# Mixture-of-experts kernel on one core: first layers of experts 1, 2 and 4 by seven products, and the weights' sums on GpSimd

## The chip, the cores and the metric

The kernel runs on one core of a Trainium2 chip. A core has five engines, each with an instruction queue of its own that it works through strictly in order: TensorE (PE in the profile, its weight loads PEld), VectorE (DVE), ScalarE (ACT), GpSimd (POOL) and SyncE (SP, which here only issues DMAs). The metric is the device time of one execution in microseconds. The result must equal the reference in float32.

## The reference, cut to what matters

```python
# attention block: r, k, v of shape (4, 8, 768, 48), w and u of shape (8, 48)
for t in range(S):
    cur = einsum('bhd,bhe->bhde', u[None] * kt, vt)
    y[:, :, t] = einsum('bhd,bhde->bhe', rt, state + cur)
    state = w[None, :, :, None] * state + einsum('bhd,bhe->bhde', kt, vt)
x = y.transpose(0, 2, 1, 3).reshape(3072, 384)          # 3072 tokens, D = 384

# experts: w_gate (384, 8), w1 (8, 384, 1024), w2 (8, 1024, 384)
for idx in argsort(-(x @ w_gate).flatten()):            # greedy, best score first
    tok, e = idx // 8, idx % 8
    if assigned[tok] < 0 and counts[e] < 384:           # each expert takes exactly 384 tokens
        assigned[tok] = e; counts[e] += 1
for e in range(8):
    h = maximum(x[assigned == e] @ w1[e], 0)            # first layer: 384 x 384 @ 384 x 1024
    out[assigned == e] = h @ w2[e]                      # second layer: 384 x 1024 @ 1024 x 384
```

## The kernel before, in words

The attention part runs first, to about 140 us, on all engines. The rest is the experts' part, and the change lies there. Every matmul is float32, and the trace shows a float32 matmul as two MATMUL records with a weight load each.

**Order of the experts.** Experts are numbered in the order in which the greedy assignment fills them up. A part of expert 0's tokens is worked on early, beside the end of the attention part; then the method `run` takes experts 1 to 7, one after the other, and the remaining tokens of expert 0 last. For each expert `run` holds `ahead`: its number, its gathered tokens, its token list, `w1` and `w2`.

**The search for the next expert.** `later()` is a generator that finds which expert is filled next and with which tokens. It is pulled in pieces by `progress`, at fixed fractions of the current expert's work (`due`), so its instructions are written in among the expert's own. It does three rounds of `count`: VectorE builds an indicator `ind` from the scores (L936), TensorE counts with it in three matmuls into `counts` (L948), VectorE reduces them to `own`, `cnt` and `wide`, one more matmul (L959) spreads the count over all partitions, and VectorE takes `most`, `full`, `dg`, `cand` and `low` from it. After the third round come the marks `acc`, their sums on TensorE (`st_ps`, L1079 and L1080), then the token lists (`some_ps`, L1412, and `list_ps`, L1430). `load_weights` has SP issue the loads of `w2` and `w1` as soon as the expert is known, and `gather` (L1518) has GpSimd issue three indirect DMAs for its tokens. `turn` (L1533) transposes the gathered tokens to `xT` on TensorE.

**First layer.** `hidden` is the plain one: 8 blocks of 128 hidden units by 3 chunks of D, 24 matmuls of 384 columns (48 in the trace), each block then passed through ScalarE's ReLU into `hid`. `hidden_by_seven` (matmuls at L1601) uses seven products instead of eight for a 2 by 2 blocking (Strassen's scheme in Winograd's form) of the first two chunks of D. For it `weight_sums` forms four sums of `w1`, `first_T1` to `first_T4` of 128 x 512 (L1548), and `row_sums` five sums of `xT`, `first_S1` to `first_S5` of 128 x 192 (L1559), all on VectorE. Inside it ScalarE copies three kinds of products out of PSUM (`keep`) and VectorE adds six pairs (`added`, each with one operand in PSUM). `FIRST_BY_SEVEN = 3, 6, 7` names the experts that use it. For such an expert the sums of `w1` are written when the expert before it stands at `t > 1.1`, that is in its second layer, and the sums of `xT` right behind the transposes.

**Second layer.** Experts 1 to 5 use `seven` (matmuls at L1698), with `seven_w2` for four sums of `w2`, `T1` to `T4` of 128 x 768 on VectorE (through `sums_of`, L1673), and `S1` to `S4` of `hid`, also through `sums_of` and of 768 elements. Experts 6 and 7 (`many`) use fifteen products, with `fifteen_w2` through `sums_of`. A third block of rows is done plainly in `result` (L1756), and `scatter` (L1750) has GpSimd write rows out by indirect DMA.

**What sets the order.** The instructions of the experts' part are put in order by a scheduler from the order in which the code is written, from what they depend on and from modelled durations; the order of each engine is then fixed. `late` is true for the first expert of `run` only: there `seven_w2` is held behind the first half's sum `S3` by `tc.issue_after`. It also goes to `hidden` as `lead`, where the first two blocks then go token block by token block.

Of the kernel before, what the change touches and what calls it, by code (L numbers as in the profile page):

```python
# [1452 lines left out]
def rwkv5_eagle_then_base_layer_balanced(  # L1453
# [12 lines left out]
    nc = tc.nc  # L1466
    N, DX = out.shape
    E, _, F = moe_w1.shape
    NT = N // 128
    CAP = N // E  # L1470
    NC = CAP // 128
# [14 lines left out]
    ADD, SUB = ALU.add, ALU.subtract  # L1486

    class Experts:
# [49 lines left out]
            *_, xT = self.turned(ahead, lambda c: self.ps_t.tile([128, KD, 128], F32, name="xT_ps"))  # L1538
            return xT

        def weight_sums(self, w1):
            H = F // 2
            at = {f"b{2 * k + f}": w1[:, k, ts(f, H)] for k in range(2) for f in range(2)}
            at.update({f"c{f}": w1[:, 2, ts(f, H)] for f in range(2)})
            for name, a, op, b in (("T1", "b1", SUB, "b0"), ("T2", "b3", SUB, "T1"), ("T3", "b3", SUB, "b1"),
                                   ("T4", "b2", SUB, "T2")):
                t = self.first.tile([128, H], F32, name=f"first_{name}")
                nc.vector.tensor_tensor(out=t, in0=at[a], in1=at[b], op=op)  # L1548
                at[name] = t
            return at  # L1550

# [110 lines left out]
        def seven_w2(self, w2):  # L1662
            H, D = KF // 2, DX // 2
            at = {f"w{2 * j + k}": w2[:, ts(j, H), ts(k, D)] for j in range(2) for k in range(2)}
            self.sums_of(at, (("T3", "w3", SUB, "w1"), ("T1", "w1", SUB, "w0"), ("T2", "w3", SUB, "T1"),
                              ("T4", "w2", SUB, "T2")), D)
            return at

        def sums_of(self, at, which, n=128):
            for name, a, op, b in which:  # L1670
                kind = f"sum_{name[0] in 'TW'}_{sum(k[0] in 'TWSH' for k in at)}"
                t = self.sums.tile([128, KF // 2, n], F32, name=name, tag=kind)
                last = nc.vector.tensor_tensor(out=t, in0=at[a], in1=at[b], op=op)  # L1673
                at[name] = t
            return last

# [85 lines left out]
            nc.scalar.copy(o_sb, o_ps)  # L1762
            self.scatter(o_sb, tok[:, c:c + 1], to)

        FIRST_BY_SEVEN = 3, 6, 7

        def run(self, ahead, later, rows, pulls={}, xT=None):
            xT, lead = xT or self.turn(ahead), True
            row_sums = weight_sums = None
            while ahead:  # L1770
                n, _, tok, w1, w2 = ahead
                nb = tok.shape[1]
                whole = nb == NC
                many = whole and n in (E - 2, E - 1)
                sums = dict(row_sums or {}, **weight_sums) if weight_sums else None
                row_sums = weight_sums = None
                ahead = next((a for a in later if a), None)
                after = ahead and ahead[0] in self.FIRST_BY_SEVEN and ahead[2].shape[1] == NC
                late, lead = lead and not many, False
                right = (self.fifteen_w2 if many else self.seven_w2)(w2) if whole and not late else None  # L1780
                left = {}
                some = pulls.get(n, 2)
                due = [1.55, 1.75] if some == 2 else [0.75 + 1.15 * i / (some - 1) for i in range(some)]

                def half(hid):
                    nonlocal right
                    for name, (i, j) in self.BLOCKS.items():
                        left[name] = hid[:, ts(j, KF // 2), ts(i, 128)]
                    if many:
                        return  # L1790
                    last = self.sums_of(left, self.SEVEN_EARLY)
                    if late:
                        with tc.issue_after(last.ins):
                            right = self.seven_w2(w2)

                def turn():
                    nonlocal xT, row_sums
                    if ahead:
                        xT = self.turn(ahead)
                        if after:  # L1800
                            row_sums = self.row_sums(xT)

                def progress(t):
                    nonlocal weight_sums
                    if after and t > 1.1 and not weight_sums:
                        weight_sums = self.weight_sums(ahead[3])
                    while due and t > due[0]:
                        due.pop(0)
                        next(later, None)
                        if many and not due:  # L1810
                            turn()

                def at_product(part):
                    progress(1 + part)

                if sums:
                    hid = self.hidden_by_seven(sums, sums, progress)
                    half(hid)
                else:
                    hid = self.hidden(w1, xT, nb * 128, half if whole else lambda hid: None, progress, late)  # L1820
                if many:
                    self.sums_of(left, self.HID_SUMS)
                    self.fifteen(left, right, tok, rows, at_product)
                    continue
                if whole:
                    self.sums_of(left, self.SEVEN_LATE)
                    self.seven(left, right, tok, rows, at_product, turn)
                for c in range(NC - 1 if whole else 0, nb):
                    if c == nb - 1 and not whole:
                        turn()  # L1830
                    self.result(c, hid, w2, tok, next(rows))
# [34 lines left out]
    with ExitStack() as whole:  # L1866
# [6 lines left out]
        with ExitStack() as part:  # L1873
# [20 lines left out]
            with tc.manual_schedule():  # L1894
                one, last = mild.run(step)
# [26 lines left out]
                ahead = 1, xg, to, *have["v"]  # L1922
# [6 lines left out]
                for m in (0, 1, 99):  # L1929
                    go(m)  # L1930
                    xT = next(turned)
# [87 lines left out]
```

## Time and profile before

| what | value |
|---|---|
| median of 3 runs | 394.73 us (394.64 to 395.28) |
| profiled execution | 393.36 us, of it 391.6 from the first to the last instruction |
| granted TensorE clock | 0.995 |
| TensorE, VectorE, ScalarE, GpSimd busy | 96%, 72%, 43%, 36% of the span |
| 0 to 140 us: the same four | 134.1, 99.1, 104.9, 90.0 us |
| 152.4 us to the end (239.2 us): the same four | 231.1, 171.8, 62.5, 47.3 us |
| first layer of experts 1 to 7 starts at | 152.4, 185.9, 218.6, 250.1, 283.2, 315.3, 344.9 us |
| rest of expert 0 starts at | 374.1 us |

The two rows by time show the two halves of the kernel: the attention part, where all engines are busy, and the experts' part, where TensorE is busy for nearly all of the time. Starts are those of the first matmul of the stage on TensorE. The profiled execution is one run of the program; the median is over other runs.

A row of the timeline reads: start, duration in us, engine, line, operation, output <- inputs, partitions x elements of one row; in brackets the idle time ahead of it and what ended that. A row of the groups or of one line's instructions has the count, shortest, median and longest duration in ns, and the first and the last start. In the waits, "VectorE own <- PE counts: 5.3, 7, 2.8" is 5.3 us in all, 7 times, 2.8 at most. In the windows each engine has its busy us and its count of instructions; behind them stand the granted clock, the share of DMA and the GB/s.

### The profile page before, as it was taken

Reading aid. Unit: us, or ns where it says so; the run is one execution under the profiler, and the core shown is the slowest. Engines: PE = TensorE matmul, PEld = TensorE weight load, DVE = VectorE, ACT = ScalarE, POOL = GpSimd, SP = SyncE. Lnnn points to the kernel's source line nnn. Section 1 sums busy time; section 2 is a strip of 40 time slices with the busy share of each in tenths; the row PEclk is TensorE's granted clock in tenths of the full one; section 3 lists DMA queues with packets and bytes.
Section 4 is the critical chain, followed back from the end, with each engine's and each line's share of the span. In section 5 each row is a group of like instructions: output and inputs, shape, how many; then the busy total and the mean of one; then the engine's idle time right before and its main releaser. Section 6 shows DMA issues by size and latency. Waiting matters only on the chain. (4 is left out here: it accounts for less than half of the span.)

```text
span 391.6 us, 9858 instructions
## 1 busy us (share of the span) xinstructions
PE 377.2 (96%) x3777; PEld 306.2 (78%) x3777; DVE 281.4 (72%) x959; ACT 169.3 (43%) x452; POOL 141.2 (36%) x173
## 2 busy tenths in 40 slices
PE   8899999999999999999999999999999999999992
PEld 7677888888877866687578899558657889989991
DVE  6755777586885788985949949888378976994530
ACT  4997989888883311312222242121222234234220
POOL 7878887767732022032122021203203212070020
PEclk9999999999999999999999999999999999999997
DMA  9999999988692164651560560109209264280010
GB/s 121 160 180 174 210 189 201 174 171 157 129 338 82 43 241 181 195 190 42 164 238 28 168 251 20 41 5 345 77 20 338 85 231 173 52 329 24 2 62 27
DMA packets 95335, 57.35 MB, mean 146 GB/s; under 512 B 77232, under 2 KB 89520, under 8 KB 95280
## 3 DMA queue, kind: packets, MB, share of 16 engines
q1 hardware_dynamic: 91936, 47.21, 48.0%
q0 software_dynamic: 3104, 9.44, 7.0%
q8 instruction: 31, 0.51, 0.6%
q14 instruction: 24, 0.20, 0.2%
q10 hardware_dynamic: 240, 0.00, 0.0%
HBM read 47.20 MB, written 9.44 MB: 145 GB/s over the span
## 5 line engine op out<-in xcount | busy, mean ns | idle before, releaser
L1624 PE MATMUL h_ps<-xT,w 128*128 128x384 f32 (+1 forms) x264 | 72.6, 427 | 0.0
L495 ACT ACTIVATE AT<-ident,dd 128x128 f32<-128x128 f32 x192 | 59.6, 392 | 2.2 <-DVE dd L448 2.1
L1624 PEld LDWEIGHTS h_ps<-xT,w 128*128 128x128 f32 x264 | 42.0, 191 | 19.6 <-issue 2.2
L1518 POOL DMA_INDIRECT xg<-x_rows,tok x22 | 22.5, 1021 | 92.4 <-PE h_ps L1624 23.7
L1750 POOL DMA_INDIRECT out_dram<-o_all,to x16 | 20.8, 1299 | 85.3 <-DVE o_all L1738 22.2
L1627 ACT ACTIVATE hid<-h_ps 128x384 f32<-128x384 f32 (+1 forms) x40 | 17.9, 449 | 54.2 <-PE h_ps L1624 50.9
L512 DVE COPY_PREDICATED AT<-mask,g_ps 64x512 f32<-64x512 uint8 (+1 forms) x48 | 32.4, 723 | 11.7 <-PE g_ps L505 9.9
L1756 PE MATMUL o_ps<-w,hid 128*128 128x384 f32 x96 | 32.5, 490 | 0.0
L505 PE MATMUL g_ps<-rT,kT 48*64 48x128 f32 (+1 forms) x768 | 26.3, 255 | 1.8 <-DVE AT L512 1.0
L436 POOL TENSOR_TENSOR kss<-krs,wk 128x384 f32<-128x384 f32 x24 | 24.3, 1016 | 8.0 <-DVE krs L340 5.0
L1756 PEld LDWEIGHTS o_ps<-w,hid 128*128 128x128 f32 x96 | 17.7, 190 | 10.6 <-issue 0.5
L545 PE MATMUL y_ps<-AT,vts 128*64 128x128 f32 x384 | 25.7, 276 | 0.0
L443 POOL TENSOR_TENSOR rk<-rk,u_bc 128x384 f32<-128x384 f32 x24 | 24.1, 1003 | 1.9
L505 PEld LDWEIGHTS g_ps<-rT,kT 48*64 48x64 f32 x768 | 20.6, 132 | 5.1 <-PE unread_ps L418 0.9
L442 POOL TENSOR_TENSOR rk<-krs 128x384 f32<-128x384 f32 x24 | 24.5, 1022 | 0.2 <-DMA krs<-in_r_dram 0.2
L545 PEld LDWEIGHTS y_ps<-AT,vts 128*64 128x64 f32 x384 | 20.6, 137 | 1.0 <-issue 0.7
L477 DVE TENSOR_TENSOR rT<-rT_ps,WR 112x512 f32<-112x512 f32 x23 | 15.7, 683 | 4.2 <-PE rT_ps L458 4.2
L448 DVE TENSOR_REDUCE dd<-rk 128x8 f32<-128x384 f32 x24 | 13.1, 545 | 6.9 <-POOL rk L443 6.9
L564 ACT COPY x<-y_ps 128x512 f32<-128x512 f32 x24 | 14.1, 586 | 5.9 <-PE y_ps L545 5.0
L458 PE MATMUL rT_ps<-ident,krs 128*112 128x128 f32 x96 | 15.4, 281 | 0.5 <-DMA krs<-in_r_dram 0.4
L1698 PE MATMUL pa_ps<-T,S 128*128 128x192 f32 x80 | 15.8, 331 | 0.0
L1729 PE MATMUL p_ps<-W,H 128*128 128x128 f32 x128 | 15.8, 275 | 0.0
(340 smaller groups left out, 834.2 us busy)
## 6 DMA issues: line engine op xcount, KB each, us to landing
w<-in_moe_w_dram SPq DMA_DIRECT2D x18, 1536.0 KB, 8.7
krs<-in_k_dram SPq DMA_DIRECT2D x24, 192.0 KB, 4.5
krs<-in_r_dram SPq DMA_DIRECT2D x24, 192.0 KB, 4.8
vts<-in_v_dram SPq DMA_DIRECT2D x24, 192.0 KB, 4.9
x_rows<-xr SPq DMA_DIRECT2D x24, 192.0 KB, 3.5
xg<-x_rows,tok POOLq DMA_INDIRECT x22, 4.0
out_dram<-o_all,to POOLq DMA_INDIRECT x16, 2.7
out_dram<-o_sb,to POOLq DMA_INDIRECT x5, 4.7
```

The source lines that it names most:

```text
L436: self.nc.gpsimd.tensor_mul(self.kss[:, n % self.NS].rearrange("p (g h) d -> p g h d", g=2)[:, :, :, 0:D], src, self.wk.rearrange("p (g h) ...
L442: nc.gpsimd.tensor_mul(rk, self.krs[:, n % self.NK, 1, 0:H, 0:D], self.krs[:, n % self.NK, 0, 0:H, 0:D])
L443: nc.gpsimd.tensor_mul(rk, rk, self.u_bc)
L495: nc.scalar.mul(AT[:, z, a, :], self.ident, dd[:, h:h + 1])
L505: nc.tensor.matmul(g_ps[ts(i, PD), z, a, i * PD:], kT[rows, a, ts(i, PD)], rT[rows, a, i * PD:], start=True, stop=True)
L512: nc.vector.copy_predicated(out=AT[keys, :, :, steps], mask=mask, data=g_ps[keys, :, :, steps])
L545: nc.tensor.matmul(yv[q * PD:(q + 1) * PD, o // 2, o % 2, :], lhsT, rhs, start=(o // 2, q) not in seen, stop=stop, skip_group_check=True)
L1518: nc.gpsimd.indirect_dma_start(out=xg[:, c, :], out_offset=None, in_=x_dram[0:within, :], in_offset=bass.IndirectOffsetOnAxis(ap=tok[:, c: ...
L1624: nc.tensor.matmul(h_ps[j][:, at], w1[:, f, ts(j, 128)], xT[:, f, at], start=(f == 0), stop=(f == KD - 1))
L1627: nc.scalar.activation(hid[:, j, 0:m], h_ps[j][:, 0:m], AF.Relu)
L1750: nc.gpsimd.indirect_dma_start(out=to, out_offset=bass.IndirectOffsetOnAxis(ap=tok, axis=0), in_=o_sb, in_offset=None)
L1756: nc.tensor.matmul(o_ps, hid[:, j, ts(c, 128)], w2[:, j, :], start=(j == 0), stop=(j == KF - 1))
```

## The change

The sums of `w2` for seven products move from VectorE to GpSimd for experts 1 to 5. Experts 1, 2 and 4 get the first layer by seven products, as experts 3, 6 and 7 have it. The sums of `w1` are made on GpSimd for experts 1 to 4, and stay on VectorE for 6 and 7. For expert 1 both kinds of sums of the first layer are written ahead of the loop. The special place of expert 1's `seven_w2` (`late`, `issue_after`) goes: its sums are written ahead of its first layer, as for the others. The lines behind L1858 stand one line higher afterwards.

```diff
--- before.py
+++ after.py
@@ -1538,14 +1538,14 @@
             *_, xT = self.turned(ahead, lambda c: self.ps_t.tile([128, KD, 128], F32, name="xT_ps"))
             return xT
 
-        def weight_sums(self, w1):
+        def weight_sums(self, w1, engine):
             H = F // 2
             at = {f"b{2 * k + f}": w1[:, k, ts(f, H)] for k in range(2) for f in range(2)}
             at.update({f"c{f}": w1[:, 2, ts(f, H)] for f in range(2)})
             for name, a, op, b in (("T1", "b1", SUB, "b0"), ("T2", "b3", SUB, "T1"), ("T3", "b3", SUB, "b1"),
                                    ("T4", "b2", SUB, "T2")):
                 t = self.first.tile([128, H], F32, name=f"first_{name}")
-                nc.vector.tensor_tensor(out=t, in0=at[a], in1=at[b], op=op)
+                engine.tensor_tensor(out=t, in0=at[a], in1=at[b], op=op)
                 at[name] = t
             return at
 
@@ -1663,14 +1663,14 @@
             H, D = KF // 2, DX // 2
             at = {f"w{2 * j + k}": w2[:, ts(j, H), ts(k, D)] for j in range(2) for k in range(2)}
             self.sums_of(at, (("T3", "w3", SUB, "w1"), ("T1", "w1", SUB, "w0"), ("T2", "w3", SUB, "T1"),
-                              ("T4", "w2", SUB, "T2")), D)
+                              ("T4", "w2", SUB, "T2")), D, nc.gpsimd)
             return at
 
-        def sums_of(self, at, which, n=128):
+        def sums_of(self, at, which, n=128, engine=nc.vector):
             for name, a, op, b in which:
                 kind = f"sum_{name[0] in 'TW'}_{sum(k[0] in 'TWSH' for k in at)}"
                 t = self.sums.tile([128, KF // 2, n], F32, name=name, tag=kind)
-                last = nc.vector.tensor_tensor(out=t, in0=at[a], in1=at[b], op=op)
+                last = engine.tensor_tensor(out=t, in0=at[a], in1=at[b], op=op)
                 at[name] = t
             return last
 
@@ -1762,11 +1762,14 @@
             nc.scalar.copy(o_sb, o_ps)
             self.scatter(o_sb, tok[:, c:c + 1], to)
 
-        FIRST_BY_SEVEN = 3, 6, 7
+        FIRST_BY_SEVEN = 1, 2, 3, 4, 6, 7
 
         def run(self, ahead, later, rows, pulls={}, xT=None):
             xT, lead = xT or self.turn(ahead), True
             row_sums = weight_sums = None
+            if ahead[0] in self.FIRST_BY_SEVEN and ahead[2].shape[1] == NC:
+                weight_sums = self.weight_sums(ahead[3], nc.gpsimd)
+                row_sums = self.row_sums(xT)
             while ahead:
                 n, _, tok, w1, w2 = ahead
                 nb = tok.shape[1]
@@ -1776,22 +1779,18 @@
                 row_sums = weight_sums = None
                 ahead = next((a for a in later if a), None)
                 after = ahead and ahead[0] in self.FIRST_BY_SEVEN and ahead[2].shape[1] == NC
-                late, lead = lead and not many, False
-                right = (self.fifteen_w2 if many else self.seven_w2)(w2) if whole and not late else None
+                late, lead = lead, False
+                right = (self.fifteen_w2 if many else self.seven_w2)(w2) if whole else None
                 left = {}
                 some = pulls.get(n, 2)
                 due = [1.55, 1.75] if some == 2 else [0.75 + 1.15 * i / (some - 1) for i in range(some)]
 
                 def half(hid):
-                    nonlocal right
                     for name, (i, j) in self.BLOCKS.items():
                         left[name] = hid[:, ts(j, KF // 2), ts(i, 128)]
                     if many:
                         return
-                    last = self.sums_of(left, self.SEVEN_EARLY)
-                    if late:
-                        with tc.issue_after(last.ins):
-                            right = self.seven_w2(w2)
+                    self.sums_of(left, self.SEVEN_EARLY)
 
                 def turn():
                     nonlocal xT, row_sums
@@ -1803,7 +1802,7 @@
                 def progress(t):
                     nonlocal weight_sums
                     if after and t > 1.1 and not weight_sums:
-                        weight_sums = self.weight_sums(ahead[3])
+                        weight_sums = self.weight_sums(ahead[3], nc.vector if ahead[0] >= E - 2 else nc.gpsimd)
                     while due and t > due[0]:
                         due.pop(0)
                         next(later, None)
```

GpSimd's order around expert 1's start, before. The gathers of `xg` are those for the early part (`e_tok`), for expert 1 and, last, for expert 2; the scatters to `out_0_dram` write the early rows (`e_o_sb`).

```order
L1518 DMA xg_2543<-x_rows,e_tok_2537 128x384 x2
L1518 DMA xg_2821<-x_rows,tok_2815 128x384 x3
L1750 DMA out_0_dram<-e_o_sb_2857,to_2848 3072x384
L1750 DMA out_0_dram<-e_o_sb_2900,to_2848 3072x384
L1518 DMA xg_3070<-x_rows,tok_3064 128x384 x3
```

The same place after the change:

```order
L1518 DMA xg_2821<-x_rows,tok_2815 128x384 x3
L1673 TENSOR_TENSOR T3_3108<-w2_2767 128x768
L1750 DMA out_0_dram<-e_o_sb_2857,to_2848 3072x384
L1673 TENSOR_TENSOR T1_3110<-w2_2767 128x768
L1673 TENSOR_TENSOR T2_3112<-w2_2767,T1_3110 128x768
L1673 TENSOR_TENSOR T4_3114<-w2_2767,T2_3112 128x768
L1750 DMA out_0_dram<-e_o_sb_2900,to_2848 3072x384
L1548 TENSOR_TENSOR first_T1_2947<-w1_2766 128x512
L1548 TENSOR_TENSOR first_T3_2951<-w1_2766 128x512
L1548 TENSOR_TENSOR first_T2_2949<-w1_2766,first_T1_2947 128x512
L1548 TENSOR_TENSOR first_T4_2953<-w1_2766,first_T2_2949 128x512
L1518 DMA xg_3088<-x_rows,tok_3082 128x384 x3
```

Between the gathers for expert 1 and those for expert 2 GpSimd now has eight sums, the four of `w2` ahead of the four of `w1`, and the two early scatters stand among them.

TensorE's order in expert 1's first layer, around the end of a count round of the search, before (the three matmuls of L948 stand just ahead of these rows, before and after):

```order
L1624 MATMUL h_ps<-xT,w_2766 128x128 x5
L959 LDWEIGHTS ones_h
L959 MATMUL counts<-wide,ones_h 128x128
L1624 MATMUL h_ps<-xT,w_2766 128x128 x2
L1624 MATMUL h_ps<-xT,w_2766 128x384 x3
L1079 LDWEIGHTS ones
L1079 MATMUL st_ps<-acc,ones 128x24
```

And after:

```order
L1601 MATMUL hb_ps<-xT,w_2766 128x192
L1601 MATMUL hb_ps<-first_S_2955,first_T_2947 128x192 x2
L1601 MATMUL h_ps<-first_S_2957,first_T_2949 128x192 x2
L1601 MATMUL h_ps<-xT,w_2766 128x192 x2
L1601 MATMUL h_ps<-first_S_2963,first_T_2951 128x192
L959 LDWEIGHTS ones_h
L959 MATMUL counts<-wide,ones_h 128x128
L1601 MATMUL h_ps<-first_S_2963,first_T_2951 128x192
```

The plain matmuls on `xT` and `w1` give way to products, and `hb_ps<-first_S,first_T` is the first that needs sums, `first_S1` and `first_T1`; the L959 count now stands behind products that wait for `first_T1`, `first_T2` and `first_T3`.

## The prediction

> **What bounds the kernel now.** I read the page first (span, busy shares, slices), then the list of waits from 150 us on, then the timeline at the places that the change touches.
>
> ```profile
> span 391.6 us, 9858 instructions
> PE 377.2 (96%) x3777; PEld 306.2 (78%) x3777; DVE 281.4 (72%) x959; ACT 169.3 (43%) x452; POOL 141.2 (36%) x173
> PE   8899999999999999999999999999999999999992
> DVE  6755777586885788985949949888378976994530
> POOL 7878887767732022032122021203203212070020
> ```
>
> TensorE is full in nearly every slice, so a microsecond that it waits is a microsecond of the span. GpSimd (POOL) is busy in the attention part, the first twelve slices, and nearly idle in the experts' part. VectorE (DVE) is not idle there: 7 to 9 tenths in most slices. What ties it to TensorE is the search for the next expert's tokens. Its counts are matmuls in TensorE's own order, fed by VectorE.
>
> ```profile
> DVE own L936 <- PE counts L948: 5.3, 7, 2.8
> DVE most L1047 <- PE counts L959: 6.0, 5, 4.3
> PEld L948 <- DVE ind L936: 2.8, 10, 0.5
> ```
>
> From 150 us on, TensorE's weight loads waited for VectorE's `ind` ten times, 2.8 us in all and 0.5 at most. The search arrives just in time: if VectorE becomes late, TensorE, which runs in order, stands at the next `L948`, `L959`, `L1079` or `L1412`.
>
> **The change, part by part.** First what it takes from TensorE. The rows are the starts of the first and second layer of experts 1, 2 (both plain) and 3 (seven products), and two runs of matmuls.
>
> ```profile
> 152.41 0.36 PE L1624 MATMUL h_ps<-xT,w 128*128 128x128 f32 x1
> 169.70 0.33 PE L1698 MATMUL pa_ps<-w,hid 128*128 128x192 f32 x1
> 185.88 0.57 PE L1624 MATMUL h_ps<-xT,w 128*128 128x384 f32 x1
> 202.25 0.41 PE L1698 MATMUL pa_ps<-w,hid 128*128 128x192 f32 x1
> 218.62 0.40 PE L1601 MATMUL h_ps<-xT,w 128*128 128x192 f32 x1
> 233.60 0.33 PE L1698 MATMUL pa_ps<-w,hid 128*128 128x192 f32 x1
> 195.72 6.61 PE L1624 MATMUL h_ps<-xT,w 128*128 128x384 f32 x20
> 219.34 1.46 PE L1601 MATMUL hc_ps<-xT,w 128*128 128x192 f32 x8
> ```
>
> Less one matmul's own 0.49 and 0.33, the runs give 0.32 us for each 384-wide and 0.16 for each 192-wide one (a float32 matmul is two in the trace). A plain first layer is 48 x 0.32 = 15.5 us, one by seven products 88 x 0.1625 = 14.3. Start to start, with the search's matmuls, expert 2 took 16.4 and expert 3 15.0. I take 1.2 us per expert, for experts 1, 2 and 4: 3.6 us less on TensorE.
>
> Now the sums. The first two rows are GpSimd's two-operand operations of the attention part (minimum, median, maximum in ns); the others what VectorE pays for what moves or is added.
>
> ```profile
> L530 POOL TENSOR_TENSOR states<-states,chunk x16: 504/506/532, 36.5 to 110.5; 128x192 f32<-128x192 f32 x16
> L443 POOL TENSOR_TENSOR rk<-rk,u_bc x24: 995/1002/1022, 8.4 to 113.0; 128x384 f32<-128x384 f32 x24
> L1673 DVE TENSOR_TENSOR T<-w x10: 948/951/959, 163.9 to 275.3; 128x768 f32<-128x768 f32 x10
> L1548 DVE TENSOR_TENSOR first_T<-w x6: 685/688/692, 201.4 to 328.9; 128x512 f32<-128x512 f32 x6
> L1559 DVE TENSOR_TENSOR first_S<-xT x9: 351/352/359, 213.3 to 344.5; 128x192 f32<-128x192 f32 x9
> ```
>
> On GpSimd 192 more elements cost 496 ns. By that line a w2 sum (768) is 506 + 3 x 496 = 1,994 ns and a w1 sum (512) 1,333. Experts 1 to 4 have four of each, 13.3 us per expert; expert 5 has four w2 sums, 8.0. VectorE loses 4 x 0.95 = 3.8 us per expert for w2 and, at expert 3, 4 x 0.69 = 2.7 for w1. Experts 1, 2 and 4 bring it row sums, 5 x 0.35 = 1.8 us each, and six `added` each, which read PSUM. [...]
>
> What decides is that the two engines stand in each other's way:
>
> ```profile
> 105.65 1.02 POOL L442 TENSOR_TENSOR rk<-krs 128x384 f32<-128x384 f32 x1
> 106.12 0.58 DVE L1177 SCALAR_TENSOR_TENSOR e_place<-e_after,e_acc 128x16 int32<-128x16 f32 x1
> 106.74 0.17 DVE L1180 TENSOR_SCALAR e_lo<-e_place 128x16 int32<-128x16 int32 x1
> 106.75 1.02 POOL L443 TENSOR_TENSOR rk<-rk,u_bc 128x384 f32<-128x384 f32 x1
> 106.82 0.98 DVE L1182 TENSOR_SCALAR e_hi<-e_place 128x16 int32<-128x16 int32 x1
> ...
> 60.20 0.52 POOL L530 TENSOR_TENSOR states<-states,chunk 128x192 f32<-128x192 f32 x1 [0.90 <-DVE states L529]
> 60.27 0.47 DVE L895 TENSOR_SCALAR top<-steps 128x8 int32<-128x8 int32 x1
> ...
> L477 DVE TENSOR_TENSOR rT<-rT_ps,WR 112x512 f32<-112x512 f32 x23 | 15.7, 683 | 4.2 <-PE rT_ps L458 4.2
> L448 DVE TENSOR_REDUCE dd<-rk 128x8 f32<-128x384 f32 x24 | 13.1, 545 | 6.9 <-POOL rk L443 6.9
> ```
>
> `e_lo` and `e_hi` are the same operation on 16 elements. `e_lo`, started before GpSimd's, took 0.17 us; `e_hi`, started 0.07 after it, took 0.98 and ended at 107.80, 0.03 after GpSimd's end at 107.77. `e_place` ended at 106.70, 0.03 after 106.67; `top` at 60.74 against 60.72. So a VectorE operation that takes two operands from SBUF, or goes from SBUF to SBUF, stands until the GpSimd operation ends. I call it closed. A reduction or one with a PSUM operand (the last two rows, mostly beside a busy GpSimd) isn't slowed: open. Between two GpSimd operations in a row one closed one gets through. [...] For the search and the `S` sums beside a 2 us sum no run here shows it yet.
>
> The price is what VectorE loses while GpSimd sums, less its idle time there. The windows are where the five groups would lie on the clock of before: behind expert 1's gathers (which end at 147.4), and for later experts when weights have landed and the sums before them are free.
>
> ```profile
> 147.70:164.00 16.30, 15.70 (x90) 11.13 (x90) 14.08 (x73) 4.04 (x9) 2.02 (x2) 1.00 0.43 144
> 173.90:189.00 15.10, 15.10 (x77) 11.06 (x76) 10.00 (x34) 3.59 (x9) 3.26 (x3) 1.00 0.12 46
> 201.40:217.00 15.60, 15.60 (x92) 12.97 (x91) 14.98 (x44) 3.45 (x9) 2.01 (x2) 1.00 0.10 37
> 230.60:246.20 15.60, 15.60 (x101) 14.11 (x100) 13.70 (x39) 4.95 (x12) 1.70 (x2) 1.00 0.08 28
> 275.30:286.00 10.70, 10.41 (x48) 6.78 (x46) 5.00 (x15) 2.95 (x7) 2.66 (x3) 1.00 0.19 68
> ```
>
> The third number after the length is VectorE's busy time. Of a search round's ten operations four are open (`own`, `cnt`, `most`, `dg`), of the sums none; I estimate 0.3 of its work as open, so a group of 13.3 us costs VectorE 0.7 x 13.3 = 9.3 us, the last 0.7 x 8.0 = 5.6. Against it stands its idle time: length less busy, plus sums that leave, less row sums. I let two thirds of that absorb the loss, since some of it is waiting for a count that TensorE has not reached. The bounds are all of it and none.
>
> - Expert 1: idle 2.2 - 1.8 - two `added`, nothing. Stall 9.3.
> - Expert 2: 5.1 + 3.8 - 1.8 = 7.1, absorbs 4.7. Stall 4.6.
> - Expert 3: 0.6 + 3.8 + 2.7 = 7.1, absorbs 4.7. Stall 4.6.
> - Expert 4: 1.9 + 3.8 - 1.8 = 3.9, absorbs 2.6. Stall 6.7.
> - Expert 5: 5.7 + 1.9 = 7.6, absorbs 5.1. Stall 0.5.
>
> The sum is 25.7 us of stalls less 3.6 = +22.1. With all idle time used the stalls are 19.1 (+15.5), with none 42.8 (+39.2).
>
> Two waits are inside this and not added. Expert 1's w1 sums stand behind its w2 sums and two scatters in GpSimd's queue:
>
> ```profile
> 147.73 1.04 POOL L1750 DMA_INDIRECT out_dram<-e_o_sb,to  x1 [0.30 <-DVE low L1034]
> w<-in_moe_w_dram SPq DMA_DIRECT2D x1, 1536.0 KB, 6.6
> w<-in_moe_w_dram SPq DMA_DIRECT2D x1, 1536.0 KB, 10.6
> ```
>
> The weights (both issued before 140 us) don't hold them up. From 147.7: four w2 sums 8.0, two scatters with the gap behind each 2.6, `first_T1` 1.3: ready at 159.6. Undelayed, TensorE needs it after 8 products of 0.325 us and 0.9 of counts, at 155.9. It would stand 3.7 us, then two more sums less a product, 2.0, for `first_T2`: 5.7. While it stands for VectorE longer than that, this is hidden. Behind GpSimd's sums also wait scatters and the next gathers, of which these are the first (for expert 2) and the fourth (for expert 5):
>
> ```profile
> 168.65 1.05 POOL L1518 DMA_INDIRECT xg<-x_rows,tok  x1 [14.72 <-PE h_ps L1624]
> 270.58 0.99 POOL L1518 DMA_INDIRECT xg<-x_rows,tok  x1 [18.55 <-PE pc_ps L1698]
> ```
>
> Each of the first four windows ends before the gather that follows it, the first by 4.6 us, so these cost nothing unless a group runs over by that much. ACT's copies in the new first layers hide as at expert 3.
>
> **Rivals.**
> 1. No exclusion for these operations: only the 5.7 us of expert 1's queue, less 3.6: +2.1, 396.8 us. Against it: every closed operation that I found starting inside a GpSimd operation ended with it. Chance 0.10.
> 2. Faster: GpSimd is quick enough. For `first_T1` to be ready at 155.9 the five sums must fit in 8.2 - 2.6 = 5.6 us, 1.1 each instead of 1.9, and nothing may be shut out; then -3.6, 391.1. From 1.9 down to 1.3 each it is still slower. The 24 equal durations of `L443` speak against. Chance 0.03.
> 3. Idle time absorbs nothing, since each search step shut out misses its place in TensorE's order: +39, 434. For it: TensorE waits already at `L948`. Against: VectorE's waits for counts (5.3 and 6.0) are slack in part. Chance 0.07.
>
> **How the numbers follow.** The profiled execution took 393.36 us, 1.76 over its span; the median is 394.73. The difference of 22.1 is put on the median: 417 us, chance 0.80, its own range 404 (were half of VectorE's work open, not 0.3, the stalls would be 6.65 + 1.95 + 1.95 + 4.05 = 14.6 us, +11.0, 405.7; I go a little lower) to 428 (two thirds of the way to no idle time used). Both ends stand for the whole, as rivals 1 to 3 outside hold 0.20. About 0.2% (0.8 us) can be told from no change: faster 0.03, same 0.02 (rival 1 with the queue shorter by 1.5 us), slower 0.95.
>
> **What would show it.** Right: GpSimd's w2 and w1 sums near 2.0 and 1.33 us; beside them VectorE rows that are 0.15 to 0.6 us today at 1 to 2 us, ending with a GpSimd sum; TensorE waiting for `ind`, `wide`, `acc` for over 20 us in all, most around expert 1; the stages of experts 1 to 3 at 36 to 40 us instead of 31.5 to 33.5, experts 5 to 7 as long as now. Wrong: VectorE's durations unchanged and one gap of some 4 us before `hb_ps<-first_S,first_T` (rival 1), or neither.

## The result, and the profile after

The changed kernel takes 436.03 us (434.46 to 436.54, 4 runs) against 394.69 us (394.39 to 395.28): a ratio of 1.104, 95% interval 1.101 to 1.107, 41.3 us slower. The forecast was 417 us, and 428 its upper end. The profiled execution has a span of 434.3 us, 42.7 more than before. First the page after: span, busy shares, and the slices, here with the granted TensorE clock in tenths.

```profile
span 434.3 us, 10177 instructions
PE 390.1 (90%) x3873; PEld 332.5 (77%) x3873; DVE 313.4 (72%) x968; ACT 177.8 (41%) x470; POOL 199.2 (46%) x209
PE   8889999999999756967995989879999999999993
...
POOL 8788877676310554096156534530380223042020
PEclk9999999999999987997998889889999999999998
```

GpSimd has 58 us more to do (the forecast came to 61). TensorE has holes in the slices from the fourteenth on. It stands idle for 44.2 us (span less busy) where it was 14.4: 29.8 us more. And it is *busy* for 12.9 us longer, though the change takes work from it. The clock row says why: it was 9 until the end before, and is 7 or 8 in several slices now.

The starts of the first layers of experts 1 to 5 (timeline of TensorE) show where the time goes:

```profile
161.15 0.41 PE L1601 MATMUL h_ps<-xT,w 128*128 128x192 f32 x1
209.19 0.41 PE L1601 MATMUL h_ps<-xT,w 128*128 128x192 f32 x1
249.54 0.41 PE L1601 MATMUL h_ps<-xT,w 128*128 128x192 f32 x1
293.11 0.41 PE L1601 MATMUL h_ps<-xT,w 128*128 128x192 f32 x1
325.04 0.54 PE L1624 MATMUL h_ps<-xT,w 128*128 128x384 f32 x1
```

| stretch | before, us | after, us | change |
|---|---|---|---|
| up to expert 1's first layer | 152.4 | 161.2 | +8.8 |
| expert 1's turn | 33.5 | 48.0 | +14.5 |
| expert 2's turn | 32.7 | 40.3 | +7.6 |
| expert 3's turn | 31.5 | 43.6 | +12.1 |
| expert 4's turn | 33.1 | 31.9 | -1.2 |
| expert 5 to the end | 108.4 | 109.3 | +0.9 |

One place in expert 1's second layer shows the whole mechanism: GpSimd's six sums, VectorE's `full` (16 elements, from SBUF to SBUF), and TensorE's next count.

```profile
188.81 1.83 POOL L1673 TENSOR_TENSOR T<-w 128x768 f32<-128x768 f32 x1
190.58 2.48 POOL L1548 TENSOR_TENSOR first_T<-w 128x512 f32<-128x512 f32 x2
193.02 1.25 POOL L1548 TENSOR_TENSOR first_T<-w,first_T 128x512 f32<-128x512 f32 x1
194.24 1.79 POOL L1673 TENSOR_TENSOR T<-w,T 128x768 f32<-128x768 f32 x1
196.00 1.25 POOL L1548 TENSOR_TENSOR first_T<-w,first_T 128x512 f32<-128x512 f32 x1
...
188.75 0.29 DVE L1047 TENSOR_REDUCE most<-counts 128x16 f32<-128x128 f32 x1 [0.31 <-issue]
189.07 8.21 DVE L1049 TENSOR_SCALAR full<-most 128x16 f32<-128x16 f32 x1
197.32 0.17 DVE L1051 TENSOR_REDUCE dg<-full 128x1 f32<-128x16 f32 x1
...
198.42 0.34 PE L948 MATMUL counts<-prop,ind 128*128 128x64 bf16 x3 [7.05 <-DVE ind L936]
```

`full` starts 0.26 us after the first sum and ends 0.03 us after the last: 8.21 us for what takes 0.17. `cand` and `ind` come from it, and TensorE stands 7.05 us for `ind`. (The search's counts are matmuls in bf16 and f16, as the rows show; not every matmul of the kernel is float32.) This is the longest case: the next longest `full`, at 162.85 us, took 3.58, and no other operation of VectorE after 145 us took over 2.5. Over the whole experts' part, `full` against the reduction `most` just ahead of it (shortest, median, longest in ns):

```profile
L1049 DVE TENSOR_SCALAR full<-most x12: 161/176/8211, 158.3 to 329.1; 128x16 f32<-128x16 f32 x12
L1047 DVE TENSOR_REDUCE most<-counts x12: 278/292/292, 158.0 to 328.8; 128x16 f32<-128x128 f32 x12
```

Then the clock. Windows of that standstill and of one in the first layer, with what follows each (the length, then TensorE's busy time; the granted clock is the third number from the end):

```profile
164.20:168.40 4.20, 0.00 (x0) 0.00 (x0) 4.13 (x6) 0.00 (x0) 3.46 (x3) 0.87 0.00 0
191.40:198.40 7.00, 0.00 (x0) 0.00 (x0) 6.93 (x6) 0.00 (x0) 5.85 (x5) 0.73 0.00 0
168.40:174.00 5.60, 5.58 (x21) 5.41 (x21) 2.46 (x10) 1.86 (x4) 0.00 (x0) 0.50 0.01 3
198.40:201.30 2.90, 2.88 (x12) 2.79 (x13) 1.16 (x5) 0.00 (x0) 1.00 (x1) 0.50 0.18 68
```

After standing 4.2 us TensorE works for 5.6 us at a clock of 0.50. In rows: the same 192-wide products, first inside that time, then at full clock.

```profile
170.64 1.49 PE L1601 MATMUL h_ps<-first_S,first_T 128*128 128x192 f32 x4
...
179.47 1.46 PE L1601 MATMUL hc_ps<-xT,w 128*128 128x192 f32 x8
```

Four take as long as eight.

### The profile page after: what moved, and what is told of

Read it like the earlier page. It is cut to its first block, busy times and chain, and to the rows that moved or that the text cites. A ratio compares the mean times of both kernels' runs of the same rounds, so it can differ in the third digit from the quotient of the medians.

```text
span 434.3 us, 10177 instructions
## 1 busy us (share of the span) xinstructions
PE 390.1 (90%) x3873; PEld 332.5 (77%) x3873; DVE 313.4 (72%) x968; ACT 177.8 (41%) x470; POOL 199.2 (46%) x209
## 4 chain that ended last, share of the span: by engine, by line
PE 57%; DVE 22%; issue 9%; POOL 4%; ACT 4%; DMA 1%; POOLq 0%; another core or an unknown queue 0%; DVEq 0%; ACTq 0%
PE h_ps L1601 8%; PE hb_ps L1601 6%; PE o_ps L1756 5%; PE pa_ps L1698 5%; PE y_ps L545 4%; PE h_ps L1624 4%; PE g_ps L505 4%; DVE full L1049 3%; PE e_h_ps L1848 3%; PE hc_ps L1601 2%; ACT AT L495 2%; DVE S L1673 2%; PE pb_ps L1698 2%; PE kT_ps L458 2%; PE x_ps L595 2%
## 5 line engine op out<-in xcount | busy, mean ns | idle before, releaser
L512 DVE COPY_PREDICATED AT<-mask,g_ps 64x512 f32<-64x512 uint8 (+1 forms) x48 | 32.5, 726 | 12.1 <-PE g_ps L505 9.9
L1756 PE MATMUL o_ps<-w,hid 128*128 128x384 f32 x96 | 33.8, 508 | 0.0
L1589 ACT ACTIVATE hid<-kept_P 128x384 f32<-128x384 f32 x36 | 18.7, 523 | 35.5 <-DVE kept_P L1593 33.9
L1756 PEld LDWEIGHTS o_ps<-w,hid 128*128 128x128 f32 x96 | 18.7, 198 | 12.1 <-issue 1.7
L545 PE MATMUL y_ps<-AT,vts 128*64 128x128 f32 x384 | 25.7, 276 | 0.0
L505 PEld LDWEIGHTS g_ps<-rT,kT 48*64 48x64 f32 x768 | 20.6, 132 | 5.1 <-ACT x L564 0.9
L1624 PE MATMUL h_ps<-xT,w 128*128 128x384 f32 (+1 forms) x96 | 22.6, 388 | 0.1
L1601 PE MATMUL h_ps<-xT,w 128*128 128x192 f32 x96 | 22.3, 353 | 0.0
L1601 PE MATMUL h_ps<-first_S,first_T 128*128 128x192 f32 x96 | 22.1, 354 | 0.0
L948 PE MATMUL counts<-prop,ind 128*128 128x64 bf16 x63 | 5.7, 202 | 17.6 <-DVE ind L936 17.6
L948 PEld LDWEIGHTS <-ind 128*128 128x128 bf16 x63 | 4.3, 103 | 22.4 <-DVE ind L936 20.7
L1673 POOL TENSOR_TENSOR T<-w,T 128x768 f32<-128x768 f32 x10 | 18.4, 1842 | 6.7 <-PE pa_ps L1698 4.5
L545 PEld LDWEIGHTS y_ps<-AT,vts 128*64 128x64 f32 x384 | 20.6, 137 | 1.0 <-issue 0.5
L1703 ACT COPY kept_P<-pa_ps 128x192 f32<-128x192 f32 x15 | 4.8, 319 | 39.9 <-PE pa_ps L1698 33.3
L1673 POOL TENSOR_TENSOR T<-w 128x768 f32<-128x768 f32 x10 | 18.2, 1823 | 5.5 <-PE pb_ps L1698 3.2
```

What stands on the lines that cost most here:

```text
L505: nc.tensor.matmul(g_ps[ts(i, PD), z, a, i * PD:], kT[rows, a, ts(i, PD)], rT[rows, a, i * PD:], start=True, stop=True)
L512: nc.vector.copy_predicated(out=AT[keys, :, :, steps], mask=mask, data=g_ps[keys, :, :, steps])
L545: nc.tensor.matmul(yv[q * PD:(q + 1) * PD, o // 2, o % 2, :], lhsT, rhs, start=(o // 2, q) not in seen, stop=stop, skip_group_check=True)
L1601: nc.tensor.matmul(ps[:, q, :], w[b][:, ts(p * Q + q, 128)], x[a], start=fresh, stop=(a, b) == pairs[-1], skip_group_check=True)
L1624: nc.tensor.matmul(h_ps[j][:, at], w1[:, f, ts(j, 128)], xT[:, f, at], start=(f == 0), stop=(f == KD - 1))
L1673: last = engine.tensor_tensor(out=t, in0=at[a], in1=at[b], op=op)
```

## The experiments

Each is timed beside runs of the kernel before, whose median was 393.5 to 394.9 us from one set of rounds to the next; ratios and differences are to the median of the same rounds. In the code, `...` marks lines left out. Theory A: VectorE's operations on SBUF are shut out while GpSimd sums, TensorE stands at the next count, and its clock then falls.

**1. The same code, all sums on VectorE.**

```diff
-                              ("T4", "w2", SUB, "T2")), D, nc.gpsimd)
+                              ("T4", "w2", SUB, "T2")), D, nc.vector)
...
-                weight_sums = self.weight_sums(ahead[3], nc.gpsimd)
+                weight_sums = self.weight_sums(ahead[3], nc.vector)
...
-                        weight_sums = self.weight_sums(ahead[3], nc.vector if ahead[0] >= E - 2 else nc.gpsimd)
+                        weight_sums = self.weight_sums(ahead[3], nc.vector)
```

> The changed kernel with all its sums of w1 and w2 back on VectorE; seven products for experts 1, 2 and 4 and the new order of the code stay. Theory A (VectorE is shut out by GpSimd's sums, TensorE stands at the next count and then runs at half clock): without sums on GpSimd the loss goes; VectorE gets about 6.5 us more work for experts 1, 2 and 4 each (2.7 sums of w1, 1.8 row sums, 2 added) against some 7 us of idle time per expert, so 388 to 402 us, near 394, with TensorE's clock at 0.99. Theory B (the new order costs: expert 1's sums stand ahead of its first layer, and the sums come late whoever makes them): 415 us or more.

400.07 us (ratio 1.013, 1.011 to 1.015). So 36 of the 41 us go with the engine that sums, and theory B, that the new order costs, falls. The page:

```profile
span 398.7 us, 10145 instructions
PE 378.1 (95%) x3873; PEld 320.8 (80%) x3873; DVE 298.4 (75%) x1004; ACT 177.8 (45%) x470; POOL 142.7 (36%) x173
```

These are the same 3873 matmuls as in the changed kernel, though not in quite the same order: the scheduler moves some of them with the sums, so some 400 places of TensorE's queue differ, and engine and order aren't fully apart here. Experiment 2 parts them. In the changed kernel TensorE stood 44.2 us and was busy 390.1; here 20.6 and 378.1. So 23.6 us of the difference are standing, and 12.0 are the same matmuls at a lower clock (0.956 against 0.990). And the time is still 5 us above before, without a sum on GpSimd: expert 1's first layer starts at 157.2 us, 4.8 late. The four sums of its `w2` stand among the search's operations on VectorE; TensorE stands 3.08 us for the count behind them and then runs at a clock of 0.50 for 3.4 us.

**2. Dead sums in the kernel before.** Nobody reads them, and the order on every other engine is the one of before. They are of 128 x 512, as `S1` to `S4` of `hid` are: the trace has those at 512 elements, not at the 768 named further up.

```diff
                     last = self.sums_of(left, self.SEVEN_EARLY)
+                    for i in range(6):
+                        dead = self.sums.tile([128, KF // 2, 128], F32, name="dead", bufs=2)
+                        nc.gpsimd.tensor_tensor(out=dead, in0=w2[:, 0:4, ts(i % 3, 128)], in1=left["S3"], op=SUB)
```

> The kernel before, with six more GpSimd sums of 128x512 (1.27 us each) in each of experts 1 to 5, back to back, of w2 and S3 into a tile that nobody reads: 38 us of GpSimd work, and no other engine's order changes. Theory A: in the changed kernel 58 us more of GpSimd went with 45 us more time (41.3 and 3.6 of saved products), 0.77 us for each; here 38 x 0.77 = 29 us, so about 424 us (410 to 435), single VectorE operations of 5 us and more, and TensorE's clock below 0.98. Theory B (only what waits for GpSimd's results is late): nobody waits for these, 394 to 397 us.

427.47 us (1.084, 1.081 to 1.086). 38.5 us of GpSimd work that nobody waits for cost 32.6 us: the theory B of this experiment, that only what waits for GpSimd's results is late, falls, and with it the order as an explanation. The page, and two places on GpSimd and VectorE:

```profile
PE 386.0 (91%) x3777; PEld 310.8 (73%) x3777; DVE 311.5 (73%) x959; ACT 168.9 (40%) x452; POOL 183.9 (43%) x203
...
164.36 10.73 POOL L1794 TENSOR_TENSOR dead<-w,S 128x512 f32<-128x512 f32 x6 [9.77 <-PE h_ps L1624]
164.50 2.02 DVE L1673 TENSOR_TENSOR T<-w 128x768 f32<-128x768 f32 x1
...
205.73 6.15 POOL L1794 TENSOR_TENSOR dead<-w,S 128x512 f32<-128x512 f32 x5
206.09 6.95 DVE L1548 TENSOR_TENSOR first_T<-w 128x512 f32<-128x512 f32 x2 [3.60 <-DMA w<-in_moe_w_dram]
```

In the first place the engines take turns: six sums of 1.28 us take 10.73, and VectorE's `T` 2.02 in place of 0.95. In the second VectorE gets in nowhere between five sums: the first of its two `first_T` took 6.35 us. The rows don't show what makes the difference. TensorE's 3777 matmuls, in the order of before, take 386.0 us in place of 377.2, and it stands 39.7 in place of 14.4: 25.3 us more of standing, and 8.8 that go with the clock (0.966 against 0.995).

**3. The same with a wait.** All six write one tile, so each waits for the one before.

```diff
-                        dead = self.sums.tile([128, KF // 2, 128], F32, name="dead", bufs=2)
+                        dead = self.sums.tile([128, KF // 2, 128], F32, name="dead", bufs=1)
```

> As the kernel with six dead sums back to back, but all six write one tile, so that each sum waits for the one before it. The work is the same and takes a little longer on GpSimd. Theory A with the refinement that a shut-out VectorE operation gets in where GpSimd itself waits: no VectorE operation stands longer than about one sum (1.3 us and 0.2), TensorE's waits stay under 3 us and its clock near 1; 400 to 415 us, at least 8 us below the one back to back. Without the refinement: as back to back, within 3 us. Theory B: 394 to 397 us.

427.63 us (1.082, 1.079 to 1.086): the same. The expectation missed; the rows show a part of it right.

```profile
205.58 7.98 POOL L1794 TENSOR_TENSOR dead<-w,S 128x512 f32<-128x512 f32 x5
...
209.01 1.75 DVE L1548 TENSOR_TENSOR first_T<-w,first_T 128x512 f32<-128x512 f32 x1
```

In this place GpSimd waits for itself, and VectorE gets in after every sum: single operations are 1.75 us long where one was 6.35, but five GpSimd sums now take 7.98 us and not 6.15. What one engine gains the other loses: here the two go one at a time, and the order of the turns doesn't change the sum. In the first place of experiment 2 the turns were taken without such waits, and there this run shows the same (10.72 us for six sums).

**4. Writing in place of reading.** Eight memsets in place of the six sums, behind a one-element copy from `S3` that ties them to the place.

```diff
                     last = self.sums_of(left, self.SEVEN_EARLY)
+                    dead = self.sums.tile([128, 1024], F32, name="dead", bufs=1)
+                    nc.gpsimd.tensor_copy(out=dead[:, 0:1], in_=left["S3"][:, 0, 0:1])
+                    for i in range(8):
+                        nc.gpsimd.memset(dead, 0.0)
```

> As the kernel with dead sums, but in place of six sums GpSimd writes zeros eight times (128x1024, 0.95 us each): the same 7.6 us for each expert, written but not read. Theory A, where it is the reading of SBUF by GpSimd that shuts out VectorE operations with two operands in SBUF: these aren't slowed, only single operand copies may be; 394 to 399 us. Theory C (any GpSimd work on SBUF shuts VectorE out): as the dead sums, 410 us or more.

396.69 us (1.005, 1.004 to 1.007). As much GpSimd time, an eighteenth of the loss. The memsets, and VectorE's sums of `w2` beside them:

```profile
L1795 POOL MEMSET dead<- x40: 951/952/1001, 164.3 to 306.4; 128x1024 f32 x40
L1673 DVE TENSOR_TENSOR T<-w x10: 951/953/959, 164.1 to 276.7; 128x768 f32<-128x768 f32 x10
```

The sums are as long as before (951), and `full` was 0.37 us at the longest. So GpSimd's being busy alone doesn't shut VectorE out here: the dead sums, which read two operands each from SBUF, cost 32.6 us, the memsets, which only write, 1.8. Long GpSimd operations that read a single operand weren't run.

**5 and 6. One kind of sum at a time.** The changed kernel with only the sums of `w2` on GpSimd (the second and third edit of experiment 1), or only those of `w1` (the first edit of it).

> The changed kernel with the sums of w1 back on VectorE; those of w2 stay on GpSimd (20 sums of 1.82 us, 36.4 us of GpSimd). From all on VectorE (400.1) to all on GpSimd (436.0) it was 35.9 us for 56.7 us of GpSimd sums, 0.63 for each. Theory A (cost goes by the GpSimd time that shuts VectorE out): 400.1 + 0.63 x 36.4 = 423 us (416 to 430), TensorE's clock 0.965 to 0.98. Theory D (the loss sits mainly in first_T arriving late for the first layers): 405 us or less.

> The changed kernel with the sums of w2 back on VectorE; those of w1 for experts 1 to 4 stay on GpSimd (16 sums of 1.27 us, 20.3 us of GpSimd). Theory A: 400.1 + 0.63 x 20.3 = 413 us (406 to 420). Theory D (first_T late): 425 us or more. The two single costs should sum to the 35.9 of both within some 6 us if each GpSimd sum costs by its own length; a half-clock cost that needs long stalls would make the sum smaller than 35.9.

421.85 us (1.074, 1.071 to 1.076) and 413.01 (1.049, 1.046 to 1.052). The expected 423 and 413 were worked out at 0.63 us for each microsecond of GpSimd sums. Above the 400.07 of all on VectorE the two cost 21.8 and 12.9, together 34.7 of the 36.0 of both; taken against the kernel before of the same rounds, 23.1 and 14.2, together 37.3 of 36.1. Either way they add up. No single late `first_T` explains the loss.

**7 and 8. Seven products without GpSimd.** The kernel before with expert 2 added, then with 2 and 4.

```diff
-        FIRST_BY_SEVEN = 3, 6, 7
+        FIRST_BY_SEVEN = 2, 3, 6, 7
```

Experiment 8 has `2, 3, 4, 6, 7`.

> The kernel before with expert 2 added to those with the first layer by seven products, all sums on VectorE and expert 1 as before. With all of 1, 2 and 4 on VectorE, expert 2's whole turn took 31.6 us against 32.7 before, and 5.3 us were lost at the start of expert 1 (4.8) and in expert 4 (1.9). Theory A (VectorE has room for expert 2's sums, and the loss was expert 1's and 4's own): 393.6 us, 393.2 to 394.2. Rival (VectorE's added work delays the search here too): 394.7 or more.

> As the kernel with expert 2 added, and expert 4 too. With 1, 2 and 4 on VectorE, expert 4's turn took 35.0 us against 33.1 before, with TensorE waiting for gathered tokens. Theory A (expert 4's loss is its own): 393.6 + 1.9 = 395.5 us (394.5 to 396.5). Rival (it came from expert 1's lateness): 392.6 us.

394.37 us against 393.58 (1.0016, 1.0007 to 1.0025), and 397.25 (1.010, 1.008 to 1.011). Both lie just above what theory A expected (394.2 and 396.5 at most). In the first, expert 2's turn is 31.6 us against 32.7, as expected, but expert 6's is 30.6 against 29.6, where TensorE waits 0.69 us for VectorE's `kept_P`, and experts 1, 3 and 4 take 0.2 to 0.4 us more each. The 1.1 us of the products are real and given back. In the second, expert 4's turn is 36.2 us, with TensorE waiting up to 2.6 us for gathered tokens: expert 4's loss is its own.

```profile
275.42 0.99 POOL L1518 DMA_INDIRECT xg<-x_rows,tok  x1 [0.55 <-PE counts L948]
...
280.01 0.90 PE L1533 MATMUL xT_ps<-ident,xg 128*128 128x128 f32 x3 [2.57 <-DMA xg<-x_rows,tok]
```

**9. More work for TensorE.** In the changed kernel, ahead of each of twelve counts:

```diff
+        for _ in range(self.warm):
+            nc.tensor.transpose(bank[:, 256:384], self.warm_by, self.warm_by)
         for j in range(NT // G):
             nc.tensor.matmul(each.rearrange("p i e -> p (i e)"),
...
```

`self.warm` is 12 from expert 2's search to expert 5's and 0 elsewhere.

> The changed kernel with 12 more float32 transposes of 128x128 on TensorE, which nobody reads, ahead of each of the 12 counts of L948 in the searches from expert 2 to 5: TensorE's work is longer by some 30 us, most of it lies where it stands for VectorE. VectorE is shut out as before. Theory A (the clock falls because TensorE stands for more than about 3 us): the granted clock goes from 0.956 to 0.975 or more and few 192-wide products take over 0.4 us; the time within 10 us of 436 (shorter where the half clock cost more than the dead work that lies outside the waits). Rival (the clock falls for another reason, such as two busy engines beside it): clock 0.95 to 0.96, products of 0.67 us as often as now, 450 us or more.

430.85 us (1.096, 1.093 to 1.098). With 144 dead transposes more the kernel loses 37.4 us to the kernel before of the same rounds, where the changed kernel lost 41.3: 4 us less. Its clock was 0.978 to 0.986 over four runs, 0.956 to 0.960 without them.

```profile
PE 397.4 (93%) x4017; PEld 340.8 (79%) x4017; DVE 312.5 (73%) x968; ACT 178.2 (42%) x470; POOL 198.4 (46%) x209
L949 PE MATMUL counts<-ident 128*128 128x128 f32 x144 | 18.4, 279 | 0.4 <-DVE most L1050 0.3
```

Without the 18.4 us of the dead work, TensorE is busy 379.0 us: 11.1 of the 12.0 us of slow clock are gone, while VectorE is busy 312.5 us, near the 313.4 of the changed kernel. So the fall of the clock goes with TensorE's standing here, not with VectorE's work.

**10. Three dead sums in place of six.** Experiment 2 with half of its work.

```diff
-                    for i in range(6):
+                    for i in range(3):
```

> The kernel before with three dead GpSimd sums back to back in each of experts 1 to 5 in place of six: 19 us of GpSimd. Six cost 32.6 us: 25.3 us more in which TensorE stands, 8.8 us more in which it is busy with the same matmuls. Theory A with the half clock (stalls under about 3 us cost no clock): half of the waits, 12 us, and 2 us or less of slower matmuls, 405 to 409 us, clock 0.985 or more. Strictly in proportion: 16.3 us, 411 us. If VectorE's idle time can take three sums of 1.27 us per expert: under 400 us.

409.59 us (1.040, 1.036 to 1.044): in proportion, and the expected discount for short standstills isn't there. In the profiled execution, the slowest of four (408.1 to 412.3 us, clocks 0.978 to 0.988), TensorE stood 11.4 us more than before and was busy 7.6 us more. A standstill of 2.50 us was followed by a clock of 0.50, though one of 2.24 us in the changed kernel (148.74 to 150.98) had left it at 1.00. The row of the first and the windows around it, then the windows around the second:

```profile
244.66 0.26 PE L948 MATMUL counts<-prop,ind 128*128 128x64 bf16 x3 [2.50 <-DVE ind L936]
...
242.63:246.04 3.41, 1.38 (x11) 1.38 (x12) 3.37 (x10) 0.29 (x1) 1.34 (x1) 1.00 0.00 0
246.04:249.46 3.42, 3.42 (x13) 3.25 (x12) 2.33 (x9) 0.03 (x1) 0.99 (x1) 0.50 0.00 0
...
146.83:150.24 3.41, 1.92 (x6) 0.77 (x5) 3.31 (x8) 0.00 (x0) 2.94 (x3) 1.00 1.03 406
150.24:153.65 3.41, 1.63 (x7) 0.85 (x8) 3.41 (x5) 0.00 (x0) 3.27 (x3) 1.00 0.46 170
153.65:157.06 3.41, 0.00 (x0) 0.00 (x0) 3.34 (x6) 0.00 (x0) 3.15 (x2) 1.00 0.00 0
157.06:160.48 3.42, 3.40 (x11) 2.39 (x11) 2.41 (x14) 0.96 (x2) 0.00 (x0) 0.50 0.00 0
```

The length of one standstill doesn't decide it: one of 2.19 us in the changed kernel (232.21 to 234.40, in a step that was busy for 1.22 of 3.41 us) was followed by 0.50. In all fourteen traces the clock changes only at whole steps of 3.41 us from its first change in that trace on; these windows are such steps. Of the 46 steps at full clock in which TensorE was busy for 46% or less, 45 were followed by the half clock (above, 1.38 of 3.41 us, 40%, and 0.00); the other, in experiment 5, had 43%. None of the 1539 busier steps was (above, 1.92 and 1.63 us, 56% and 48%). The standstill of 2.50 us lay mostly in one step; the one of 2.24 us was split between two.

**11 and 12. Only expert 5's sums of `w2` on GpSimd,** in the kernel before, with expert 4 added to `FIRST_BY_SEVEN`, then with expert 2.

```diff
...
-                right = (self.fifteen_w2 if many else self.seven_w2)(w2) if whole and not late else None
+                right = None
+                if whole and not late:
+                    right = self.fifteen_w2(w2) if many else self.seven_w2(w2, nc.gpsimd if n == 5 else nc.vector)
...
-        FIRST_BY_SEVEN = 3, 6, 7
+        FIRST_BY_SEVEN = 3, 4, 6, 7
```

Experiment 12 has `2, 3, 6, 7`. Left out is the engine as an argument of `seven_w2` and `sums_of`.

> The kernel before, with expert 4 added to those with the first layer by seven products (sums of w1 on VectorE), and of all sums only expert 5's four of w2 on GpSimd, where in the changed kernel they lay between 315 and 323.5 us with VectorE nearly idle. In the changed kernel expert 4's turn was 31.9 us against 33.1 before; with all sums on VectorE it was 35.0. Theory A (GpSimd's sums cost only where VectorE has work that TensorE waits for; here they take 3.8 us off VectorE for nothing): 392.5 us, 1.1 less than before. Rival 1 (they shut VectorE out here too, since its order differs): 396 or more. Rival 2 (expert 4 loses to its gathers as with all sums on VectorE): 395 to 396.

> As the kernel with expert 2 added (394.37 us), with expert 5's four sums of w2 on GpSimd. Theory A: the sums shut out little in this place, and VectorE gets 3.8 us of room: 394.4 us or up to 0.5 less. Rival (7.3 us of GpSimd sums at the 0.63 us each of the changed kernel): 398 to 399 us.

399.17 us (1.010, 1.009 to 1.012) and 394.75 (1.000, 0.999 to 1.001). In the second the four sums lie beside the plain rows that end expert 4's turn and cost nothing that can be told. In the first, one of them stood in GpSimd's queue ahead of the gathers, waiting for `w2` to land:

```profile
272.51 1.84 POOL L1673 TENSOR_TENSOR T<-w 128x768 f32<-128x768 f32 x1 [19.58 <-DMA w<-in_moe_w_dram]
274.51 1.00 POOL L1518 DMA_INDIRECT xg<-x_rows,tok  x1 [0.15 <-issue]
...
277.76 0.55 PE L1533 MATMUL xT_ps<-ident,xg 128*128 128x128 f32 x3 [1.94 <-DMA xg<-x_rows,tok]
```

The gathers came 4 us later than the 270.58 of before, and TensorE waited for the tokens. But in experiment 8, without a sum on GpSimd, they came at 275.42, and expert 4's move alone cost 2.9 us (experiment 8 against 7). The rival of the expectation, that expert 4 loses to its gathers whoever sums, so may explain the larger part of the 4.5 us lost here; what the sum in the queue adds isn't shown, since this version with all sums on VectorE wasn't run. No version beat the kernel before.

## Why the prediction was right and wrong

- **Right: the bound and the sign.** TensorE waits for the search, VectorE for GpSimd. Reductions stayed at 0.29 us, `full` went to 8.21. The turns of experts 1 to 3 took 48.0, 40.3 and 43.6 us, where 36 to 40 was the sign, and the later ones are as long as before. Most of the holes are waits for `ind`, `wide` and `acc` (us in all, times, longest; the first was 2.8, 10, 0.5):

```profile
PEld L948 <- DVE ind L936: 20.3, 8, 7.3
PE counts L959 <- DVE wide L936: 8.3, 4, 4.5
PE st_ps L1079 <- DVE acc L1075: 2.7, 1, 2.7
```

- **Wrong: a term was missing.** The step "a microsecond that it waits is a microsecond of the span", and with it the sum of 25.7 us of stalls less 3.6, is the one that failed. The microseconds in which TensorE stood cost more, since the clock was at 0.50 for a time behind many of the standstills: 12.0 us in the changed kernel (experiments 1 and 9). The 42.7 us of the span are 23.6 of standing that goes with the engine that sums, 6.2 of standing that stays without it, these 12.0, and 0.9 by which TensorE's busy time in experiment 1 is over that of before, where 3.6 less was forecast. A hint stood in the trace before. TensorE idles behind its last matmul there, and the clock is at 0.64:

```profile
386.00:391.60 5.60, 0.00 (x0) 0.00 (x0) 0.00 (x0) 0.00 (x0) 0.68 (x1) 0.64 0.12 41
```

- **Mis-sized: the stalls, 25.7.** TensorE stands 29.8 us more than before, of which 23.6 go with the engine that sums and 6.2 remain with all sums on VectorE in their new places (experiment 1). The total is near, the parts aren't: GpSimd's groups ahead of expert 1's and 2's first layers (9.3 and 4.6, 13.9 forecast) cost 23.3 with the clock and the 4.8 of the new places, the group in expert 2's turn 7.6 against 4.6, the one in expert 3's 12.1 against 6.7. (The measured changes of expert 1 and 2 are net of what the products save there, 1.1 us for expert 2; the forecasts are not.) Expert 5's was right: 0.5 forecast, nothing seen, and nothing in experiment 12 either.
- **Right in part: "one closed one gets through".** Six sums in a row shut `full` out for all their length, five a `first_T` (experiment 2). Elsewhere the engines took turns, with waits between the sums (experiment 3) and in one place without them; what decides isn't shown. By experiment 3 the turns change no time.
- **Wrong: the 3.6 us saved.** 1.1 us per expert is there (experiment 7) but returned at once, and expert 1's own move costs 4.8 (experiment 1).
- **Sizes of the sums.** They took 1.81 and 1.27 us; the line through the attention part's rows gave 1.99 and 1.33.
- **Rival 3** (434 us, chance 0.07) has nearly the measured time, but not its reason: it had 42.8 us of stalls and no clock, where 29.8 and 12.9 were measured. Rivals 1 and 2 fall with experiment 2.

The range failed for the same reason: both ends were made of stalls alone.

## What to carry to other kernels

Beside the sums moved to GpSimd, VectorE's reductions and its operations with an operand in PSUM took their usual time here (started inside a sum of the changed kernel, `most` took 0.28 and 0.29 us, `own` 0.21 to 0.22, one pair of `added` 0.55); with its SBUF-to-SBUF work the sums took turns (four `full` 1.13 to 8.21 us in place of 0.17), and the price was set by what waited for VectorE in that place: 0.63 us for each microsecond of sums in the changed kernel, 0.85 in experiment 2 (32.6 on 38.5), and nothing to be told in experiment 12. For a kernel that TensorE bounds, an estimate from these runs adds a quarter to two thirds to the standstills (3.7 on 14.8 and 2.9 on 9.9 in experiments 5 and 6 against 1; 8.8 on 25.3, 12.0 on 23.6, 7.6 on 11.4 in 2, 1 and 10): the matmuls behind many of them ran at a clock of 0.50 for a step of 3.41 us or more. Holes that left TensorE busy for over 46% of each step cost no clock here (experiment 10).

## What the runs showed of the hardware

Dead work can pay: 144 transposes that nobody reads, put where TensorE stood, shortened the changed kernel by 4 us: TensorE's own work took 11.1 us less. In all fourteen traces the clock changed at steps of 3.41 us and went with TensorE's busy share in them, not with the length of one gap (2.19 us was followed by 0.50, 2.24 us was not): it was at 0.50 behind 45 of the 46 full-clock steps that were busy for 46% or less, and behind none of the 1539 busier ones (experiment 10). And eight memsets as long as six sums on GpSimd cost an eighteenth of what the sums cost, 1.8 us against 32.6.
